# Attention and MLP in one kernel: attention's PSUM in two pools, one copy for eight half transposes, scores in two tasks

## The chip, the cores and the metric

The kernel runs on one core of a Trainium2 chip. The metric is the time of one execution on the device, in microseconds, as the median of three runs. TensorE (PE) multiplies and transposes into PSUM; VectorE (DVE) and ScalarE (ACT) read PSUM; GpSimd (POOL) works in SBUF only; SyncE (SP) issues the DMAs.

## The reference

Causal attention by blocks of 64 over 8 batches, 8 heads, 576 positions and 64 channels, followed by layer norm and a two-layer MLP with ReLU and a residual, all in float32.

```python
scores = scale * np.matmul(q, k.transpose(0, 1, 3, 2))
mask = block_i >= block_j                      # blocks of 64
attn = softmax(np.where(mask, scores, -1e9))   # rows, sum + 1e-9
x = np.matmul(attn, v).transpose(0, 2, 1, 3).reshape(B, S, H * D)
xn = (x - mu) / np.sqrt(var + 1e-06) * g_ln
return x + np.maximum(xn @ w_ch1, 0.0) @ w_ch2
```

## The kernel before

**Tiling.** Attention works on 32 pairs of heads (`pair(k)`). Of a pair's 576 positions the first 64 are done apart, for eight pairs together (`first(m)`, four times). The other 512 make four query blocks of 128, numbered 1 to 4, whose keys reach to 64(2i+1) columns: 192, 320, 448 and 576. Blocks 1 and 2 form the low part, blocks 3 and 4 the high part.

**One pair, step by step** (lines of the profile). `scores1` multiplies the low blocks of both heads into two PSUM tiles `s1` of 512 columns; `scores0` the high blocks into two tiles `s` of 1024 columns, `sab` (L426). `soften` (L444) has VectorE add the mask, scale and take the row minimum out of PSUM into SBUF (`pu` for the low blocks, `pab` for the high ones), and ScalarE the exponential with its sum (L447). `turn` (L457) has TensorE transpose eight cells of 128 x 128 in halves of 64 rows: 16 instructions, the upper halves into one `tr` tile, the lower into another. A pair has three such groups: one from `pu`, two from `pab` (h = 0 and 1). `turned_to` copies each of the two tiles (512 columns) to SBUF as `pt`, by an instruction that the planner gives to VectorE (L237) or ScalarE (L235). `pv` (L469, L473) multiplies with the values into a PSUM tile `o` of 512 columns, in two steps: 4.5 for the low part, 5 for the high one. VectorE transposes `o` out (L536, the output read-out).

**PSUM.** One pool, tag `tr`, has four tiles of one bank that `tr`, `s1`, `o` and later the products `p` share. The other has two tiles `s` of two banks, and gives its place to the second layer's `y` when attention is over.

**Order.** A planner (`Plan`) goes through all tasks in an assumed time, with costs from tables, and gives each free engine the ready task with the lowest priority number; what it emits is the order on the chip, where each engine takes its instructions strictly in that order. For TensorE's part of attention the order is fixed by hand: `pe(at, phase, ...)` files a task under a pair and a phase, and `plan.chain` strings them up by these numbers. Transposes and value steps of pair k stand at k + 1, behind the scores of pair k + 1. `TURN` is the planner's cost of two half transposes.

**The rest of the work.** Beside attention run the decoding of the weights (`decode`, L351 to L379: ScalarE, VectorE, GpSimd and DMAs), layer norm of the first tiles (`norm_tiles`) and the making of the MLP's operands. After attention the MLP follows in 5 rounds of 8 groups: seven products (`products`, L873) and the second layer (`second`, L935) for each.

Of the kernel before, what the change touches and what calls it, by code (L numbers as in the profile page):

```python
# [26 lines left out]
TURN = .112  # L27
# [31 lines left out]
class Plan:  # L59
# [34 lines left out]
    def run(self):  # L94
# [27 lines left out]
        while events:  # L122
# [19 lines left out]
            for eng, heap in ready.items():  # L142
# [3 lines left out]
                while heap:  # L146
# [28 lines left out]
                    k.eng, k.cost, k.done = eng, cost, True  # L175
# [27 lines left out]
def attn_mlp_kernel(ctx: ExitStack, tc: tile.TileContext, qk, qk0, v, v0, w1, w2, g, out):  # L203
# [18 lines left out]
    psum = ctx.enter_context(tc.tile_pool(name="psum", bufs=1, space=PSUM))  # L222
# [802 lines left out]
```

## Time and profile before

| | us |
|---|---|
| three runs | 1059.27, 1056.75, 1055.28 |
| median | 1056.75 |
| profiled execution | 1059.55 |
| its span, first to last instruction | 1057.5 |
| TensorE busy in the span | 1019.6 |
| VectorE, ScalarE, GpSimd busy | 752.7, 515.0, 292.1 |

The profile gives each instruction's start and duration, and for idle time the engine that ended it. A matmul's recorded duration includes its way through the array, so the next one starts before it ends: what a group costs TensorE is the distance from its first start to the next group's first start. The same holds, to a lesser degree, on VectorE and ScalarE.

### The profile page before, as it was taken

Reading aid. Unit: us, or ns where it says so; the run is one execution under the profiler, and the core shown is the slowest. Engines: PE = TensorE matmul, PEld = TensorE weight load, DVE = VectorE, ACT = ScalarE, POOL = GpSimd, SP = SyncE. Lnnn points to the kernel's source line nnn. Section 1 sums busy time; section 2 is a strip of 40 time slices with the busy share of each in tenths; the row PEclk is TensorE's granted clock in tenths of the full one; section 3 lists DMA queues with packets and bytes.
Section 4 is the critical chain, followed back from the end, with each engine's and each line's share of the span. In section 5 each row is a group of like instructions: output and inputs, shape, how many; then the busy total and the mean of one; then the engine's idle time right before and its main releaser. Section 6 shows DMA issues by size and latency. Waiting matters only on the chain.

```text
span 1057.5 us, 19502 instructions
## 1 busy us (share of the span) xinstructions
PE 1019.6 (96%) x7032; PEld 835.2 (79%) x7032; DVE 752.7 (71%) x1636; ACT 515.0 (49%) x1251; POOL 292.1 (28%) x476
## 2 busy tenths in 40 slices
PE   8998998978999999999999999999999999999998
PEld 6776776756677888878888888888888888888997
DVE  6979899988888887894665694665585565465554
ACT  7989898779784643441433251343242422222221
POOL 0323355525245754440222250222231120000000
PEclk9999999989999999999999999999999999999999
DMA  8778798878779999757687657678657767426873
GB/s 273 252 250 261 201 283 260 237 229 300 253 230 311 324 294 270 225 206 255 206 255 219 185 219 256 186 225 263 182 172 260 239 185 237 156 110 233 308 279 125
DMA packets 238688, 248.98 MB, mean 235 GB/s; under 512 B 159488, under 2 KB 189184, under 8 KB 228352
## 3 DMA queue, kind: packets, MB, share of 16 engines
q1 hardware_dynamic: 238592, 247.74, 72.6%
q8 instruction: 55, 0.90, 0.3%
q14 instruction: 41, 0.34, 0.1%
HBM read 182.68 MB, written 65.01 MB: 234 GB/s over the span
## 4 chain that ended last, share of the span: by engine, by line
PE 74%; DVE 12%; ACT 5%; DMA 4%; issue 3%; POOL 2%; SPq 1%; DVEq 0%; POOLq 0%; ACTq 0%
PE y L935 35%; PE p L873 31%; PE o L473 4%; ACT pu L447 2%; DVE pab L444 2%; PE o L469 2%; PE s L426 2%; ACT pt L235 1%; DMA wcs<-wd 1%; DVE pt L237 1%; DVE pu L444 1%; DMA raw<-qk 1%; DVE sgn L360 1%; DVE xm L771 1%; PE tr L457 1%
## 5 line engine op out<-in xcount | busy, mean ns | idle before, releaser
L935 PE MATMUL y<-wc,h 128*128 128x512 f32 (+1 forms) x1740 | 434.5, 388 | 0.9 <-DVE h L893 0.8
L935 PEld LDWEIGHTS y<-wc,h 128*128 128x128 f32 x1740 | 323.0, 188 | 67.3 <-DVE h L893 2.5
L947 DVE TENSOR_TENSOR ya<-y,ya 128x512 f32<-128x512 f32 x290 | 197.9, 684 | 188.9 <-PE y L935 186.7
L873 PE MATMUL p<-xm,wa 128*128 128x512 f32 (+1 forms) x960 | 222.3, 368 | 0.5 <-ACT pt L235 0.5
L873 PEld LDWEIGHTS p<-xm,wa 128*128 128x128 f32 x960 | 169.7, 188 | 32.3 <-ACT pt L235 0.8
L873 PE MATMUL p<-xm,wb 128*128 128x512 f32 (+1 forms) x720 | 166.8, 368 | 0.0
L892 ACT ACTIVATE h<-t 128x512 fp32r<-128x512 f32 (+1 forms) x120 | 62.2, 579 | 175.5 <-DVE t L886 175.4
L881 ACT COPY t<-p 128x512 f32<-128x512 f32 (+1 forms) x120 | 65.3, 544 | 167.0 <-PE p L873 166.8
L873 PEld LDWEIGHTS p<-xm,wb 128*128 128x128 f32 x720 | 127.5, 188 | 23.8 <-issue 0.2
L886 DVE TENSOR_TENSOR t<-p,t 128x512 f32<-128x512 f32 (+1 forms) x120 | 76.3, 636 | 45.9 <-PE p L873 40.9
L426 PE MATMUL s<-raw 64*128 64x224 f32 (+3 forms) x768 | 96.4, 388 | 0.8 <-DVE nm L444 0.5
L447 ACT ACTIVATE pab<-pab,nm 128x576 f32<-128x576 f32 (+1 forms) x128 | 91.5, 723 | 1.1 <-DVE nm L444 0.9
L426 PEld LDWEIGHTS s<-raw 64*128 64x128 f32 x768 | 74.9, 188 | 16.2 <-issue 5.0
L444 DVE CUSTOM_DVE_ANT_0 pab<-s,never 128x576 f32<-128x576 f32 (+1 forms) x128 | 83.4, 682 | 3.0 <-PE s L426 2.3
L473 PE MATMUL o<-pt,v 128*64 128x256 f32 (+1 forms) x768 | 83.2, 352 | 0.0
L473 PEld LDWEIGHTS o<-pt,v 128*64 128x64 f32 x768 | 60.3, 141 | 26.2 <-issue 3.2
L893 DVE SCALAR_TENSOR_TENSOR h<-t,h 128x512 fp32r<-128x512 f32 (+1 forms) x120 | 75.8, 681 | 4.5 <-ACT h L892 4.5
L447 ACT ACTIVATE pu<-pu,nm 128x192 f32<-128x192 f32 (+1 forms) x128 | 63.8, 500 | 30.1 <-DVE nm L444 28.6
L687 POOL TENSOR_SCALAR norm<-norm 128x1 f32<-128x1 f32 x28 | 8.0, 287 | 251.5 <-ACT xn L684 248.9
L457 PE MATMUL tr<-ident,pab 64*128 64x64 f32 x1024 | 53.2, 230 | 24.3 <-ACT pt L235 18.7
L235 ACT COPY pt<-tr 128x512 f32<-128x512 f32 x135 | 71.2, 581 | 2.6 <-PE tr L457 1.2
L354 POOL TENSOR_SCALAR mag<-mag 128x512 f32<-128x512 f32 x32 | 49.9, 1564 | 77.5 <-ACT mag L351 71.7
(95 smaller groups left out, 1027.6 us busy)
## 6 DMA issues: line engine op xcount, KB each, us to landing
wc<-wcs SPq DMA_DIRECT2D x40, 1024.0 KB, 7.0
wa<-was SPq DMA_DIRECT2D x32, 1024.0 KB, 6.6
wb<-wbs SPq DMA_DIRECT2D x32, 768.0 KB, 5.5
raw<-qk SPq DMA_DIRECT2D x31, 576.0 KB, 5.0
wr<-w SPq DMA_DIRECT2D x32, 512.0 KB, 6.2
v<-v SPq DMA_DIRECT2D x32, 320.0 KB, 4.9
x<-xd SPq DMA_DIRECT2D x144, 64.0 KB, 3.8
xrow<-x SPq DMA_DIRECT2D x36, 256.0 KB, 4.0
```

Source lines behind the costliest of these rows:

```text
L235: e.copy(out=out, in_=in_)
L426: nc.tensor.matmul(x, raw.t[HALF[h], 0, col], raw.t[HALF[h], 1, at:at + x.shape[1]], start=True, stop=True)
L444: add("DVE", dve(n) + .01, lambda: nc.vector.tensor_tensor_reduce(out=two(p.t[:, part(i, h)]), in0=mine(), in1=two(hide), scale=-0.125, sc ...
L447: add("ACT", act(n, True) + .14, lambda: nc.scalar.activation(out=p.t[:, part(i, h)], in_=p.t[:, part(i, h)], func=AF.Exp, bias=nm.t[:, at ...
L457: nc.tensor.transpose(to.t[:, 64 * n:64 * n + 64], x[rows], ident[rows, rows])
L473: nc.tensor.matmul(o.t[HALF[h], at + lo:at + 256], v_sb.t[:, ck, HALF[h]], rhs(h), start=False, stop=(n == len(steps) - 1), skip_group_che ...
L873: nc.tensor.matmul(x.t[:, 0:TN], w_(l), xs[m].t[:, 0:half, o, k], start=start and k == e == 0, stop=k == 1 and e == 2, skip_group_check=True)
L881: add("ACT", act(TN), lambda: nc.scalar.copy(out=t.t[:, 0:TN], in_=x.t[:, 0:TN]), r=[r], w=[new], prio=0)
L886: add("DVE", dve(TN), lambda: nc.vector.tensor_add(t.t[:, 0:TN], x.t[:, 0:TN], t.t[:, 0:TN]), r=r, w=[new], prio=0)
L893: add("DVE", dve(TN), lambda: nc.vector.scalar_tensor_tensor(out=x.t[:, 1, 0:TN], in0=src(), scalar=0.0, in1=x.t[:, 0, 0:TN], op0=ALU.max, ...
L935: nc.tensor.matmul(yb.t[:, cut], x.t[:, l, at:at + P], wc.t[:, i, o, cut], start=i == e == 0, stop=i == 1 and e == 2, skip_group_check=end)
L947: add("DVE", dve(cut.stop - cut.start), lambda yb=yb, ya=ya, cut=cut: nc.vector.tensor_add(ya.t[:, cut], yb.t[:, cut], ya.t[:, cut]), r=[p ...
```

## The change

**PSUM.** The pool `tr` becomes `turns`, two tiles of two banks, for `tr`, `s1` and `o`; it lies on the right side of PSUM, the two `s` tiles (`banks`) on the left. `s1` is one tile of 1024 columns with a half for each head. A `tr` tile takes a whole group: the upper halves in its first bank, the lower in its second. `o` uses the first bank of its tile alone. After attention `p` follows on the left and `y` on the right.

**Copies.** `turned_to` empties a group with one instruction of 1024 columns in place of two of 512.

**Scores and order.** `scores0` is split into `scores4` (block 4, 576 columns) and `scores3` (block 3, 448 columns), each of them across both `s` tiles: block 4 takes columns 224 to 800, block 3 those outside. The reductions come in the order 4, 4, 3, 3. The phases are now in `ORDER`: scores of the low blocks, transposes of the former pair's `pu`, block 4, the former pair's two groups of `pab`, block 3; then the value steps as before. `TURN` falls from .112 to .063. `first` takes double tiles likewise, with the same instructions.

```diff
-TURN = .112
+TURN = .063
+ORDER = {"1": 0, "u": 0.1, "4": 0.2, "a": 0.3, "b": 0.4, "3": 0.5}
...
-    psum = ctx.enter_context(tc.tile_pool(name="psum", bufs=1, space=PSUM))
...
-    banks = tc.tile_pool(name="banks", bufs=1, space=PSUM)
-    new_s = kind("s", [P, 1024], F32, 2, banks.__enter__())
+    def region(name, side):
+        return tc.tile_pool(name=name, bufs=1, space=PSUM, side=side)
+    banks = region("banks", "left"), region("turns", "right")
+    new_s = kind("s", [P, 1024], F32, 2, banks[0].__enter__())
 
     class Again:
 
 
-        pool = None
+        def __init__(self, n):
+            self.n, self.pool = n, None
 
         def tile(self, *args, **kw):
             if self.pool is None:
-                banks.__exit__(None, None, None)
-                self.pool = ctx.enter_context(tc.tile_pool(name="banks_y", bufs=1, space=PSUM))
+                banks[self.n].__exit__(None, None, None)
+                self.pool = ctx.enter_context(region(f"again{self.n}", ("left", "right")[self.n]))
             return self.pool.tile(*args, **kw)
-    new_y = kind("y", [P, 512], F32, 4, Again())
+    new_p = kind("p", [P, 512], F32, 4, Again(0))
+    new_y = kind("y", [P, 512], F32, 4, Again(1))
     steps = {}
-    new_tr, new_s1, new_o, new_p = (kind(n, [P, 512], F32, 4, psum, "tr") for n in ("tr", "s1", "o", "p"))
+    turns = banks[1].__enter__()
+    new_tr, new_s1, new_o = (kind(n, [P, 1024], F32, 2, turns, "tr") for n in ("tr", "s1", "o"))
...
-                    for rows, to in zip(HALF, o):
-                        nc.tensor.transpose(to.t[:, 64 * n:64 * n + 64], x[rows], ident[rows, rows])
+                    for z, rows in enumerate(HALF):
+                        nc.tensor.transpose(o.t[:, 512 * z + 64 * n:512 * z + 64 * n + 64], x[rows], ident[rows, rows])
             return go
 
         def turned_to(pt, at, o, x, to):
-            for q, src in enumerate(o):
-                x.append(Buf(parent=pt))
-                evac(lambda q=q: to()[..., 64 * q:64 * q + 64],
-                     lambda src=src: src.t.rearrange("p (c i q) -> p c i q", c=4, q=64), 512, r=[src], w=[x[-1]], prio=at)
+            x.append(Buf(parent=pt))
+            evac(lambda: to().rearrange("p n (z q) -> p z n q", z=2),
+                 lambda: o.t.rearrange("p (z n q) -> p z n q", z=2, q=64), 1024, r=[o], w=[x[-1]], prio=at)
...
-        s1 = [new_s1(), new_s1()]
+        s1 = new_s1()
         nm = new_nm()
         pu = new_pu()
 
         def scores1():
-            a, b = (x.t for x in s1)
+            a, b = s1.t[:, 0:512], s1.t[:, 512:1024]
             mm(2, a[:, 0:320], b[:, 0:320])
             mm(1, a[:, 320:512], b[:, 320:512])
-        pe(k, 0, 512 * 4 / 2400 + .04, scores1, r=[early], w=s1, prio=pr(), mode=64)
+        pe(k, ORDER["1"], 512 * 4 / 2400 + .04, scores1, r=[early], w=[s1], prio=pr(), mode=64)
         low = [[], []]
-        for h, s in enumerate(s1):
-            for n, (i, lo, hi) in enumerate(((2, 0, 320), (1, 320, 512))):
-                low[h].append(soften(pu, s, nm, 4 + 2 * h + n, i, h, lo))
+        for h in range(2):
+            for n, (i, lo) in enumerate(((2, 0), (1, 320))):
+                low[h].append(soften(pu, s1, nm, 4 + 2 * h + n, i, h, 512 * h + lo))
 
         sab = [new_s(), new_s()]
         pab = big_of[k, 0] = new_pab()
 
-        def scores0():
+        def scores4():
             a, b = (x.t for x in sab)
             mm(4, a[:, 224:512], b[:, 224:512])
             mm(4, a[:, 512:800], b[:, 512:800], skip=288)
+
+        def scores3():
+            a, b = (x.t for x in sab)
             mm(3, a[:, 0:224], b[:, 0:224])
             mm(3, a[:, 800:1024], b[:, 800:1024], skip=224)
-        pe(k, 1, 1024 * 4 / 2400 + .06, scores0, r=[early, late], w=[*sab, ends.setdefault(k, Buf())], prio=pr(), mode=64)
+        s4, s3 = [Buf(parent=x) for x in sab], [Buf(parent=x) for x in sab]
+        pe(k, ORDER["4"], 576 * 4 / 2400 + .03, scores4, r=[early, late], w=s4, prio=pr(), mode=64)
+        pe(k, ORDER["3"], 448 * 4 / 2400 + .03, scores3, r=[early, late], w=[*s3, ends.setdefault(k, Buf())], prio=pr(), mode=64)
         done = [[], []]
-        for h, s in enumerate(sab):
-            for n, i in enumerate((4, 3)):
-                done[h].append(soften(pab, s, nm, 2 * h + n, i, h, 224))
+        for n, i, s in (0, 4, s4), (1, 3, s3):
+            for h in range(2):
+                done[h].append(soften(pab, s[h], nm, 2 * h + n, i, h, 224))
         pt0 = big_of[k, 1] = new_pt0()
         final[k] = [*done[0], *done[1]]
         got = []
 
         for h in range(2):
-            o = [new_tr(), new_tr()]
+            o = new_tr()
             cells = [x for c in range(3) for x in ((3, h, c + 1), (4, h, c + 1))] + [(3 + h, h, 0), (4, h, 4)]
             slots = lambda cells=cells: [pab.t[:, cell(*x)] for x in cells]
             need = [*done[h], done[1 - h][1 - h]]
-            pe(k + 1, 3, 8 * TURN, turn(o, slots), r=list(dict.fromkeys(need)), w=o, alloc=[pt0], prio=pr(), mode=64)
-            turned_to(pt0, pr(), o, got, lambda h=h: pt0.t[:, h])
+            pe(k + 1, ORDER["ab"[h]], 8 * TURN, turn(o, slots), r=list(dict.fromkeys(need)), w=[o], alloc=[pt0], prio=pr(), mode=64)
+            turned_to(pt0, pr(), o, got, lambda h=h: pt0.t[:, h].rearrange("p c i n -> p (c i) n"))
...
-        o = [new_tr(), new_tr()]
+        o = new_tr()
         cells = [x for h in range(2) for x in ((1, h, 1), (2, h, 1), (1 + h, h, 0), (2, h, 2))]
         slots = lambda: [pu.t[:, cell(*x)] for x in cells]
-        pe(k + 1, 2, 8 * TURN, turn(o, slots), r=[*low[0], *low[1]], w=o, alloc=[pt1], prio=pr(), mode=64)
-        turned_to(pt1, pr(), o, got, lambda: pt1.t.rearrange("p h c i n -> p (h c) i n"))
+        pe(k + 1, ORDER["u"], 8 * TURN, turn(o, slots), r=[*low[0], *low[1]], w=[o], alloc=[pt1], prio=pr(), mode=64)
+        turned_to(pt1, pr(), o, got, lambda: pt1.t.rearrange("p h c i n -> p (h c i) n"))
...
-        add("DVE", dve(512), lambda: nc.vector.transpose(ot.t, ob.t), r=part_o, w=[ot], prio=pr())
+        add("DVE", dve(512), lambda: nc.vector.transpose(ot.t, ob.t[:, 0:512]), r=part_o, w=[ot], prio=pr())
...
-        s, e, nm = [new_tr(), new_tr()], new_e0(), new_nm()
+        s, e, nm = new_tr(), new_e0(), new_nm()
...
-        o, ot, ots = [new_o(), new_o()], new_ot0(), []
+        o, ot, ots = new_o(), new_ot0(), []
```

Lines of the new kernel stand five to nine below the old ones: L431 is the scores, L462 the transposes, L473 and L477 the value steps, L449 the reductions, L545 the output read-out, L882 the products.

TensorE, pair 7, from its scores to the first value step of pair 6. `s_1019`, `s_1020` and `s_953` are `s1` tiles; `s` are the tiles of the high blocks; `x4` counts equal rows. Before:

```order
L426 MATMUL s_1019<-raw 128x320
L426 MATMUL s_1020<-raw 128x320
L426 MATMUL s_1019<-raw 128x192
L426 MATMUL s_1020<-raw 128x192
L426 MATMUL s<-raw 128x288 x4
L426 MATMUL s<-raw 128x224 x4
L457 MATMUL tr<-ident,pu 128x64 x16
L457 MATMUL tr<-ident,pab 128x64 x32
L469 MATMUL o<-pt_1052,v 64x256 x2
```

and now:

```order
L431 MATMUL s_953<-raw 128x320 x2
L431 MATMUL s_953<-raw 128x192 x2
L462 MATMUL tr<-ident,pu 128x64 x16
L431 MATMUL s<-raw 128x288 x4
L462 MATMUL tr<-ident,pab 128x64 x32
L431 MATMUL s<-raw 128x224 x4
L473 MATMUL o<-pt_967,v 64x256 x2
```

The scores of block 4 and block 3 now stand on the two sides of the former pair's `pab` transposes, and the `pu` transposes ahead of both.

The same place now, with the semaphores that each row waits for (Activation is ScalarE), from block 4 to the first value step:

```order
L431 MATMUL s<-raw 128x288 x4
L462 MATMUL tr<-ident,pab 128x64 [waits DVE_49,Activation_49]
L462 MATMUL tr<-ident,pab 128x64 x11
L462 MATMUL tr<-ident,pab 128x64 [waits Activation_49]
L462 MATMUL tr<-ident,pab 128x64 x3
L462 MATMUL tr<-ident,pab 128x64 [waits Activation_49]
L462 MATMUL tr<-ident,pab 128x64 x15
L431 MATMUL s<-raw 128x224 [waits DVE_49] x2
L431 MATMUL s<-raw 128x224 x2
L473 MATMUL o<-pt_967,v 64x256 [waits DMAHW4_49,Activation_49]
```

The first two rows of block 3 (64 x 224) wait for VectorE, which reads block 4 in the same tiles; the value step waits for a ScalarE copy.

VectorE, from pair 7's high reductions (`pab`) to the output read-out (L536). The `ISA nm` rows read the minimum out. Before:

```order
L444 ISA pab,nm<-s,never 128x576
L444 ISA nm 128x1
L444 ISA pab,nm<-s,never 128x448
L444 ISA nm 128x1
L444 ISA pab,nm<-s,never 128x448
L444 ISA nm 128x1
L237 COPY pt_1079<-tr 128x8x64
L444 ISA pab,nm<-s,never 128x576
L444 ISA nm 128x1
L237 COPY pt_1079<-tr 128x8x64
L536 STREAM_TRANSPOSE ot<-o 128x512
```

and now:

```order
L449 ISA pab,nm<-s,never 128x576
L449 ISA nm 128x1
L449 ISA pab,nm<-s,never 128x576
L449 ISA nm 128x1
L237 COPY pt_1003<-tr 128x2x8x64
L449 ISA pab,nm<-s,never 128x448
L449 ISA nm 128x1
L449 ISA pab,nm<-s,never 128x448
L449 ISA nm 128x1
L365 SCALAR_TENSOR_TENSOR sgn<-wr,sgn 128x512
L368 SCALAR_TENSOR_TENSOR sgn<-mag,sgn 128x512
L545 STREAM_TRANSPOSE ot<-o 128x512
```

Two copies of one bank stood behind three or four of the reductions; one copy of two banks now stands between the two reductions of 576 and the two of 448 columns. The output read-out follows behind them as before, here with two decoding steps (L365, L368) ahead of it.

TensorE at the end of attention, from pair 31's last scores. Before:

```order
L426 MATMUL s<-raw 128x224 x4
L457 MATMUL tr<-ident,pu 128x64 x16
L457 MATMUL tr<-ident,pab 128x64 x16
L873 MATMUL p<-xm_2150,wa 128x512 x6
L457 MATMUL tr<-ident,pab 128x64 x16
L469 MATMUL o<-pt_4731,v 64x256 x2
L473 MATMUL o<-pt_4731,v 64x256 x2
L473 MATMUL o<-pt_4731,v 64x128 x2
```

and now:

```order
L431 MATMUL s<-raw 128x224 x4
L882 MATMUL p<-xm_2069,wa 128x512 x6
L473 MATMUL o<-pt_4440,v 64x256 x2
L477 MATMUL o<-pt_4440,v 64x256 x2
L477 MATMUL o<-pt_4440,v 64x128 x2
L473 MATMUL o<-pt_4477,v 64x256 x2
L477 MATMUL o<-pt_4477,v 64x256 x6
L477 MATMUL o<-pt_4477,v 64x128 x2
L462 MATMUL tr<-ident,pu 128x64 x16
```

The first product `p` stood between two groups of `pab` transposes; it now stands straight behind block 3 of pair 31 and ahead of pair 30's value steps.

## Rows read from the trace of the kernel before

**Rows 1.** The page's busy times: us, share of the span, instructions, by engine.

```profile
PE 1019.6 (96%) x7032; PEld 835.2 (79%) x7032; DVE 752.7 (71%) x1636; ACT 515.0 (49%) x1251; POOL 292.1 (28%) x476
```

**Rows 2.** Busy time by stretch: stretch, length, PE, PEld, DVE, ACT, POOL, clock, DMA, GB/s.

```profile
18.50:299.30 280.80, 250.56 (x3290) 196.14 (x3288) 246.47 (x725) 238.66 (x658) 108.22 (x139) 0.98 0.80 253
299.30:322.30 23.00, 22.50 (x222) 16.17 (x220) 18.79 (x40) 17.61 (x42) 13.60 (x10) 1.00 0.74 235
322.30:1057.50 735.20, 730.83 (x3388) 610.58 (x3384) 477.13 (x836) 246.14 (x519) 169.58 (x322) 1.00 0.70 228
```

**Rows 3.** TensorE's timeline (start, us, instructions): scores of pair 2 and pair 31.

```profile
18.50 2.86 PE L426 MATMUL s<-raw 64*128 64x320 f32 x24
...
299.31 2.86 PE L426 MATMUL s<-raw 64*128 64x320 f32 x24
```

**Rows 4.** TensorE's timeline, one undisturbed pair; idle time before and releaser in brackets.

```profile
101.01 2.86 PE L426 MATMUL s<-raw 64*128 64x320 f32 x24
103.70 0.66 PE L457 MATMUL tr<-ident,pu 64*128 64x64 f32 x16
104.20 0.67 PE L457 MATMUL tr<-ident,pab 64*128 64x64 f32 x16
105.50 0.27 PE L457 MATMUL tr<-ident,pab 64*128 64x64 f32 x1 [0.64 <-ACT pt L235]
105.99 0.70 PE L457 MATMUL tr<-ident,pab 64*128 64x64 f32 x15 [0.21 <-ACT pt L235]
106.62 0.65 PE L469 MATMUL o<-pt,v 128*64 128x256 f32 x4
...
107.78 0.65 PE L469 MATMUL o<-pt,v 128*64 128x256 f32 x4
...
109.87 0.69 PE L574 MATMUL tr<-qk 64*64 64x64 f32 x32
```

**Rows 5.** TensorE's waits, 18.5 to 299.3 us: us in total, times, longest.

```profile
PE tr L457 <- ACT pt L235: 18.1, 37, 3.6
PE o L469 <- ACT pt L235: 4.0, 11, 0.7
PE tr L457 <- DVE nm L444: 2.9, 6, 0.7
```

**Rows 6.** Timeline of all engines, two stretches: VectorE's reductions, decoding, copies.

```profile
28.53 0.49 DVE L444 CUSTOM_DVE_ANT_0 pu<-s,never 128x320 f32<-128x320 f32 x1 [0.34 <-PE s L426]
...
29.91 0.69 DVE L360 SCALAR_TENSOR_TENSOR sgn<-wr,sgn 128x512 int32<-128x512 int32 x1
...
30.51 0.75 DVE L444 CUSTOM_DVE_ANT_0 pab<-s,never 128x576 f32<-128x576 f32 x1
...
115.93 0.75 DVE L444 CUSTOM_DVE_ANT_0 pab<-s,never 128x576 f32<-128x576 f32 x1
...
116.61 0.62 DVE L444 CUSTOM_DVE_ANT_0 pab<-s,never 128x448 f32<-128x448 f32 x1
...
117.70 0.69 DVE L237 COPY pt<-tr 128x512 f32<-128x512 f32 x1
...
118.30 0.75 DVE L444 CUSTOM_DVE_ANT_0 pab<-s,never 128x576 f32<-128x576 f32 x1
```

**Rows 7.** The same timeline: ScalarE's copies and exponentials.

```profile
104.89 1.52 ACT L235 COPY pt<-tr 128x512 f32<-128x512 f32 x3
...
107.08 0.58 ACT L235 COPY pt<-tr 128x512 f32<-128x512 f32 x1
...
108.21 0.77 ACT L447 ACTIVATE pab<-pab,nm 128x576 f32<-128x576 f32 x1
...
108.97 0.67 ACT L447 ACTIVATE pab<-pab,nm 128x448 f32<-128x448 f32 x1
...
109.62 0.68 ACT L351 ACTIVATE mag<-wr 128x512 f32<-128x512 f32 x1
```

**Rows 8.** VectorE's longest wait, 18.5 to 299.3 us: us in total, times, longest.

```profile
DVE ot L536 <- PE o L473: 28.1, 17, 4.1
```

More of the change, by code (lines that the diff above doesn't have):

```diff
@@ L174, in run @@
                         cost, mode = cost + SWITCH[k.mode], k.mode
-                    k.eng, k.cost, k.done = eng, cost, True
+                    k.eng, k.cost, k.done, k.t0 = eng, cost, True, now
                     fn()
@@ L574, in first @@
         pe(8 * m + 4, -1, .6, lambda: by_quarter(lambda a, u, f, t, cols, at: nc.tensor.matmul(
-            s[u].t[t, at], q0.t[f, a, 0], q0.t[f, a, 1], start=True, stop=True, skip_group_check=True)),
-            r=[q0], w=s, alloc=[e], prio=pr(), mode=2)
+            s.t[t, 512 * u + at.start:512 * u + at.stop], q0.t[f, a, 0], q0.t[f, a, 1], start=True, stop=True, skip_group_check=True)),
+            r=[q0], w=[s], alloc=[e], prio=pr(), mode=2)
         load(P * 2048, lambda: nc.sync.dma_start(out=v_0.t.rearrange("p (a n) -> p a n", n=64), in_=v0[m]), w=[v_0], prio=prio)
@@ L582, in first @@
             add("DVE", dve(256), lambda u=u: nc.vector.tensor_reduce(
-                out=nm.t[:, 4 * u:4 * u + 4], in_=ev(s[u].t[:, 0:256]), op=ALU.max, axis=AX.X), r=[s[u]], w=[m1], prio=pr())
-            add("DVE", dve(256), lambda u=u, bc=bc: nc.vector.tensor_sub(side(u), ev(s[u].t[:, 0:256]), bc()),
-                r=[s[u], m1], w=[d1], prio=pr())
+                out=nm.t[:, 4 * u:4 * u + 4], in_=ev(s.t[:, 512 * u:512 * u + 256]), op=ALU.max, axis=AX.X), r=[s], w=[m1], prio=pr())
+            add("DVE", dve(256), lambda u=u, bc=bc: nc.vector.tensor_sub(side(u), ev(s.t[:, 512 * u:512 * u + 256]), bc()),
+                r=[s, m1], w=[d1], prio=pr())
             d.append(d1)
@@ L604, in first @@
         pe(8 * m + 5, 2.5, 4 * .112, across, r=[pn], w=[tr], alloc=[pt], prio=pr())
-        evac(lambda: pt.t, lambda: tr.t, 512, r=[tr], w=[turned_], prio=pr())
-        o, ot, ots = [new_o(), new_o()], new_ot0(), []
+        evac(lambda: pt.t, lambda: tr.t[:, 0:512], 512, r=[tr], w=[turned_], prio=pr())
+        o, ot, ots = new_o(), new_ot0(), []
         def values():
@@ L614, in values @@
                         nc.tensor.matmul(
-                            o[u].t[HALF[h], 0:256].rearrange("p (t c q) -> p t c q", t=2, q=32)[:, :, c],
+                            o.t[HALF[h], 512 * u:512 * u + 256].rearrange("p (t c q) -> p t c q", t=2, q=32)[:, :, c],
                             v_0.t[HALF[u], at], pt.t[HALF[u], at].rearrange("p (t q) -> p t q", q=32), start=True, stop=True,
                             skip_group_check=True)
-        pe(8 * m + 5, 5.5, .6, values, r=[turned_, v_0], w=o, alloc=[ot], prio=pr(), mode=2)
+        pe(8 * m + 5, 5.5, .6, values, r=[turned_, v_0], w=[o], alloc=[ot], prio=pr(), mode=2)
         for u in range(2):
             ots.append(Buf(parent=ot))
-            add("DVE", dve(256), lambda u=u: nc.vector.transpose(half(ot, u), o[u].t[:, 0:256]), r=[o[u]], w=[ots[u]], prio=pr())
+            add("DVE", dve(256), lambda u=u: nc.vector.transpose(half(ot, u), o.t[:, 512 * u:512 * u + 256]), r=[o], w=[ots[u]], prio=pr())
         x0parts[m] = []
```

## The prediction

> **What bounds the kernel now.** I read the page's busy table first (TensorE 96%, the others far less [rows 1]), then the busy time by stretch, then TensorE's rows of one undisturbed pair, its waits, and last the rows of VectorE and ScalarE that release it. The run has two stages. From 322 us on TensorE is busy for 730.8 of 735.2 us [rows 2] with the products and second-layer sums, which the edit leaves as they are; nothing is to be won there. The attention stage is where TensorE is held up. Scores of pair 2 start at 18.50 us and of pair 31 at 299.31 us; 30 such rows, so 29 periods of 280.8 / 29 = 9.68 us on average [rows 3]. Of these 29 distances 11 are up to 9.0 us, 8 more up to 9.6, and 10 longer.
>
> In an undisturbed pair [rows 4] the scores take 103.70 - 101.01 = 2.69 us of issue, 16 transposes 0.50 us (103.70 to 104.20), the two value steps 1.16 us (106.62 to 107.78) and 2.09 us (107.78 to 109.87). With three groups of transposes that is 2.69 + 1.50 + 1.16 + 2.09 = 7.44 us of work in a period of 8.86: 1.42 us are lost, all of them between 104.70 and 106.62, where the second `pab` group waits for copies out of PSUM. The waits say the same of the whole stage: 18.1 us of transposes waiting for ScalarE's copies, 4.0 us of value steps waiting for them, 2.9 us for VectorE's reductions [rows 5].
>
> But TensorE is not alone. In the same 280.8 us it is busy 250.6 us, VectorE 246.5 and ScalarE 238.7 [rows 2]: 8.64, 8.50 and 8.23 us a period. So three engines at 85 to 89% hold each other up, and a TensorE stall that goes is worth only what the other two can follow.
>
> **The change, part by part.** I call the groups of transposes u (from `pu`), a and b (from `pab`), and the scores s1, s4 (576 columns) and s3 (448).
>
> *One copy in place of two.* Three ScalarE copies of 512 take 1.52 us together, one alone 0.58 [rows 7], so they follow each other every (1.52 - 0.58) / 2 = 0.47 us; an exponential of 576 columns is followed after 0.76 us (108.21 to 108.97) and one of 448 after 0.65 (to 109.62) [rows 7], 0.11 us for 128 columns. A copy of 1024 is then an estimated 0.47 + 4 x 0.11 = 0.91 us, against 0.94 for two. VectorE: a 512 copy takes 0.60 us from its start to the next, the 576 reduction 0.68 and each 448 one 0.545 [rows 6]; at about 1.05 ns a column, 1024 is about 1.13 us against 1.20. The program's lists hold 131 ScalarE and 61 VectorE copies before, 71 and 25 after. ScalarE: 131 x 0.47 = 61.6 to 71 x 0.91 = 64.6 us, no gain. VectorE: 61 x 0.60 = 36.6 to 25 x 1.13 = 28.3 us, a gain of 8.3 us, 0.26 us a pair. The 1024 source spans two banks; the 576 reduction does so already (columns 224 to 800 of its tile), at the rate of the 448 one, so I add nothing for that. The copy starts later, after all 16 transposes, and lasts 0.91 to 1.13 us where two copies ran side by side in about 0.6; that costs about 0.4 us at each place where TensorE is next in line.
>
> *The new order hides that.* Per column the scores take 2.69 / 1536 = 1.75 ns, so s1 is 0.90, s4 1.01 and s3 0.78 us. Put a pair together by hand, t = 0 when s1(k) starts. s1 to 0.90, u to 1.40, s4 to 2.41. VectorE reads out the former pair's output from 0.1 to 0.8 (512 columns, counted as a 512 copy with its hand-over; it stands ahead of the reductions in the order), starts the four `pu` reductions at 1.10 when s1 has ended, is through at 2.48 (four take 29.91 - 28.53 = 1.38 us [rows 6]) and releases s1's banks at 2.6. a then runs 2.6 to 3.1: 0.2 us lost. ScalarE copies u from 1.6 to 2.5, so b has its banks at 3.1 and runs to 3.6. s3 writes the outer columns of the two banks whose inner columns the two 576 reductions read; the order shows it waiting for VectorE there. These run from 2.6 to 4.0, so s3 is held from 3.6 to 4.05: 0.45 us lost, and ends at 4.83. ScalarE's copy of a (3.5 to 4.4) and VectorE's of b (4.05 to 5.2) are both done when the value steps want them (4.83 and 5.99), which end at 8.08. So 1.42 us of loss becomes 0.64, and 8.86 becomes 8.08.
>
> *What keeps that from coming through whole.* ScalarE needs 8.23 us a period and loses no work, so an undisturbed pair cannot run below about 8.25: the 11 short periods gain 0.6 us each, 6.6 us. The 8 middle ones, with VectorE or ScalarE late by less than an operation, I give 0.5 us: 4.0. The 10 long ones are filled by other work on VectorE (layer norm, weight decoding, the first-block task) and gain what VectorE itself sheds, 0.26 us: 2.6. Together 13.2 us.
>
> *The two pools.* s1, the transposes and the output share two double banks instead of four single ones, so the output tile, which needs one bank, now holds two, and u waits for the former pair's output to be read out. In the hand schedule that is done at 0.8, before u is due at 0.90, so it costs nothing; if VectorE is one operation late (0.60 us for a decoding step, from 29.91 to 30.51 [rows 6]) it costs 0.5 us in that pair. The middle periods' 0.5 us, in place of 0.78, already allow for such a delay in every second one.
>
> *The end of attention.* Products now live where the scores were, so the first product must wait until pair 31's last 448 reductions are read, and the order puts it straight behind s3(31), ahead of the value steps that could run: two reductions of 0.545 us and about 0.3 us of hand-over, 1.4 us lost. Before, that stretch lost 0.5 us in all (22.50 busy of 23.00 [rows 2]). I take 1.4 lost; the bounds are 0.5 (later gaps shrink by as much) and 3 (a copy ahead of the reductions).
>
> *Nothing else.* The first-block task gets a double tile for each pair of single ones: same instructions, four times in all. Changes of tile shape on TensorE stay at two a pair, since s1 to s3 and all transposes use 64 rows. TensorE's granted clock was 0.98 in the stage [rows 2]; fewer stalls might win back the 2%, at most some 2.5 us of its 250 us of work if half of it lies beside other waits; I take nothing.
>
> **The sum** is made against the profiled execution, 1059.55 us (its span 1057.5 and about 2 us around it): 1059.55 - 13.2 + 1.4 = 1047.7. The median of the three runs, 1056.75, lies 2.8 us below that execution, so 1047.7 - 2.8 = 1045 us, a gain of 1.1%.
>
> **Rivals.**
> 1. *The rest follows too, 1033 us.* If the removed stalls also shorten the middle and long periods by 0.78, the gain is 29 x 0.78 = 22.6 us, plus 2 us of clock, less 1.4: 1056.75 - 23.2 = 1033.5. For it: VectorE stood still for 28.1 us of the stage with the output read-out waiting for value steps [rows 8], which is slack. Against it: ScalarE's 8.23 us a period.
> 2. *ScalarE is the bound, 1054 us.* Its work does not shrink, and at 85% busy with waits on both sides it may already set the mean. Then only a part of the 8.3 us that VectorE sheds shows, say a third: 1056.75 - 2.8 = 1054. Against it: in the undisturbed pair TensorE waits for ScalarE in one burst, not all along.
> 3. *VectorE's queue drives TensorE, 1070 us.* The place is the loop output read-out, four reductions, two 576 reductions, copy of b, value step: by the schedule 5.2 + 2.09 = 7.3 us if nothing else sits in it, since s3 can no longer be written while its banks are read. VectorE's other work averages 8.50 - 0.26 - 4.5 (0.60 + 1.38 + 1.36 + 1.13) = 3.7 us a pair, of which 1.1 is the 448 reductions. Whatever of it is queued inside that loop is paid by TensorE. It decides from 9.68 - 7.3 = 2.4 us a pair; at 2.85 us it costs 0.45 x 29 = 13 us: 1070. Against it: the order mostly puts decoding after the 448 reductions, where TensorE is in the value steps. No row here shows TensorE writing to a bank that another engine reads. The Trainium skill, "PSUM — Partial Sum Buffer", section "PSUM bank collisions raise a hardware error", says to guard PSUM by bank, not by address: two engines in one bank at once is an error, whatever the columns. By that rule splitting the scores over the same two banks gives no early write, and the time is this rival's 1070; if s3 could run beside the reductions, this rival would lose its loop and half its chance.
>
> **How the numbers follow.** Forecast 50% (1037 to 1051), rival 1 15% (1027 to 1037), rival 2 15% (1051 to 1058), rival 3 20% (1061 to 1080). A measurement of this kernel tells about 0.5% from no change, 5.3 us, so faster means below 1051.5: 50 + 15 and a fifth of rival 2, 68%. Within 0.5% is the rest of rival 2, 12%; slower 20%. The range leaves out 5% below and 15% above: 1029 to 1064. Its lower end is rival 1 with more clock regained, its upper end the start of rival 3.
>
> **What would show it.** In the profile of the changed kernel: 30 rows of s1 at a mean distance of 9.2 us; in an undisturbed pair a short wait (0.2 us) of a, one of s3 for VectorE's reductions (0.45 us), and none of the value steps; transposes waiting for ScalarE's copies down from 18 us to under 6; copies of 1024 at about 1.0 us (ScalarE) and 1.2 us (VectorE) recorded; VectorE's copies 8 us less in all; a wait of 1 to 2 us ahead of the first product. I am wrong if the waits of u, a and s3 for VectorE add up to more than the 25 us they replace (rival 3), if ScalarE shows no idle time in the stage (rival 2), or if the products' stage, 735 us, does not simply move forward because its weights or rows come late.

## The result: 1.0% faster, and the profile after

The changed kernel takes 1046.23 us (median of four runs, 1045.03 to 1046.90) against 1056.37 us for the kernel before on the same chip: ratio 0.9899, 95% interval 0.9877 to 0.9921. Its profiled execution has a span of 1044.7 us, 12.8 us shorter than before. TensorE's work is the same, VectorE is busy 8.0 us less [rows 1]:

```profile
PE 1018.1 (97%) x7032; PEld 819.9 (78%) x7032; DVE 744.7 (71%) x1607; ACT 515.9 (49%) x1188; POOL 288.2 (28%) x472
```

The same three stretches as in [rows 2], cut at the scores of pair 2 and of pair 31 (stretch, length, PE, PEld, DVE, ACT, POOL, clock, DMA, GB/s), and the two rows of TensorE's timeline that answer to [rows 3]:

```profile
17.42:280.40 262.98, 247.82 (x3290) 179.66 (x3288) 234.76 (x687) 235.60 (x599) 96.49 (x128) 0.99 0.82 260
280.40:304.20 23.80, 22.45 (x224) 16.54 (x222) 18.11 (x38) 16.56 (x35) 11.61 (x11) 1.00 0.65 235
304.20:1044.70 740.50, 733.21 (x3384) 612.11 (x3382) 481.69 (x848) 251.53 (x525) 179.44 (x329) 1.00 0.71 230
```

```profile
17.42 1.14 PE L431 MATMUL s<-raw 64*128 64x320 f32 x8
...
280.40 1.13 PE L431 MATMUL s<-raw 64*128 64x320 f32 x8
```

Pair 2 starts 1.1 us earlier, the 29 periods last 263.0 us where they lasted 280.8, and from the scores of pair 31 to the end it is 764.3 us where it was 758.2: 1.1 + 17.8 - 6.1 = 12.8 us. Attention gained more than the whole kernel, and a third of that was lost behind it.

TensorE's timeline of an undisturbed pair (its period is 70.27 - 61.96 = 8.31 us), as [rows 4]:

```profile
61.96 1.13 PE L431 MATMUL s<-raw 64*128 64x320 f32 x8
62.93 0.66 PE L462 MATMUL tr<-ident,pu 64*128 64x64 f32 x16
63.42 1.19 PE L431 MATMUL s<-raw 64*128 64x288 f32 x8
64.76 1.22 PE L462 MATMUL tr<-ident,pab 64*128 64x64 f32 x32
65.78 1.38 PE L431 MATMUL s<-raw 64*128 64x224 f32 x8
67.09 0.65 PE L473 MATMUL o<-pt,v 128*64 128x256 f32 x4
...
70.27 1.13 PE L431 MATMUL s<-raw 64*128 64x320 f32 x8
...
74.08 1.02 PE L431 MATMUL s<-raw 64*128 64x224 f32 x8
75.03 0.65 PE L473 MATMUL o<-pt,v 128*64 128x256 f32 x4
```

No row has an idle time in brackets, yet two groups were held. Block 3's scores take 67.09 - 65.78 = 1.31 us here and 75.03 - 74.08 = 0.95 in the next pair: the wait for the second 576 reduction lies between the matmuls of the group, and only the distance to the next group shows it. TensorE's waits from 18 to 290 us (in total, times, longest), as [rows 5]:

```profile
PE tr L462 <- DVE nm L449: 5.8, 8, 1.8
PE tr L462 <- DVE e L593: 2.1, 4, 0.7
PE s L431 <- DVE ot L545: 1.9, 6, 0.7
PE p L882 <- DVE nm L449: 1.2, 1, 1.2
...
PE tr L462 <- ACT pt L235: 0.9, 4, 0.4
```

The 18.1 us of transposes waiting for ScalarE's copies are 0.9 us. Of the 6.1 us lost later 0.8 lie in the second stretch (23.80 us in place of 23.00), in which the first product waits 1.2 us. The other 5.3 us have one place, the end of the MLP's first round. The timeline of all engines there:

```profile
447.17 1.29 DVE L780 TENSOR_TENSOR xm<-xt,xm 128x256 fp32r<-128x256 f32 x2
...
448.38 0.95 DVE L769 TENSOR_TENSOR tt<-xt,tt 128x256 f32<-128x256 f32 x1
...
449.25 1.55 DVE L237 CAST xm<-tt 128x256 fp32r<-128x256 f32 x2
...
450.73 3.47 DVE L902 SCALAR_TENSOR_TENSOR h<-t,h 128x512 fp32r<-128x512 f32 x3
...
453.12 4.63 PE L944 MATMUL y<-wc,h 128*128 128x512 f32 x10 [3.55 <-DVE h L902]
```

The second layer waits 3.55 us for `h`, which stands on VectorE behind steps that make the second round's operands. The stretches of the wait and of the ten matmuls behind it:

```profile
450.50:453.10 2.60, 0.00 (x0) 0.00 (x0) 2.60 (x4) 0.19 (x1) 2.60 (x4) 0.85 0.93 394
453.10:457.55 4.45, 4.43 (x10) 3.44 (x11) 4.45 (x8) 1.41 (x4) 4.05 (x5) 0.50 0.50 212
```

The ten run at a granted clock of 0.50, 443 ns each where six took 1.36 us, 227 ns each, before the wait: 2.2 us more. The clock stays at 0.50 up to 459.1 us, and four products behind them start 427 ns apart as well, some 0.8 us more.

### The profile page after: what moved, and what is told of

The parts are those of the page before. It is cut to its first block, busy times and chain, and to the rows that moved or that the text cites. A ratio compares the mean times of both kernels' runs of the same rounds, so it can differ in the third digit from the quotient of the medians.

```text
span 1044.7 us, 19419 instructions
## 1 busy us (share of the span) xinstructions
PE 1018.1 (97%) x7032; PEld 819.9 (78%) x7032; DVE 744.7 (71%) x1607; ACT 515.9 (49%) x1188; POOL 288.2 (28%) x472
## 4 chain that ended last, share of the span: by engine, by line
PE 82%; DVE 8%; ACT 3%; SPq 2%; DMA 2%; issue 2%; POOL 1%; DVEq 0%; POOLq 0%; ACTq 0%
PE y L944 37%; PE p L882 32%; PE o L477 4%; PE s L431 4%; PE tr L462 3%; ACT pt L235 2%; PE o L473 2%; DVE pab L449 2%; SPq L675 1%; DVE pu L449 1%; DMA v<-v 1%; DVE ot L545 1%; DMA wcs<-wd 1%; DMA x<-xd 0%; ACT pab L452 0%
## 5 line engine op out<-in xcount | busy, mean ns | idle before, releaser
L882 PE MATMUL p<-xm,wa 128*128 128x512 f32 (+1 forms) x960 | 222.1, 369 | 1.2 <-DVE nm L449 1.2
L882 PEld LDWEIGHTS p<-xm,wa 128*128 128x128 f32 x960 | 170.5, 189 | 33.3 <-DVE nm L449 1.6
L882 PE MATMUL p<-xm,wb 128*128 128x512 f32 (+1 forms) x720 | 166.3, 368 | 0.0
L882 PEld LDWEIGHTS p<-xm,wb 128*128 128x128 f32 x720 | 127.5, 188 | 23.9 <-DVE t L895 0.2
L431 PE MATMUL s<-raw 64*128 64x288 f32 (+3 forms) x768 | 115.4, 401 | 3.4 <-DVE ot L545 1.9
L452 ACT ACTIVATE pab<-pab,nm 128x448 f32<-128x448 f32 (+1 forms) x128 | 90.7, 712 | 2.3 <-DVE nm L449 2.2
L431 PEld LDWEIGHTS s<-raw 64*128 64x128 f32 x768 | 73.6, 190 | 20.3 <-issue 4.1
L449 DVE CUSTOM_DVE_ANT_0 pab<-s,never 128x448 f32<-128x448 f32 (+1 forms) x128 | 82.9, 685 | 7.1 <-PE s L431 6.4
L235 ACT COPY pt<-tr 128x1024 f32<-128x1024 f32 (+1 forms) x75 | 73.7, 985 | 22.3 <-PE tr L462 20.8
L477 PE MATMUL o<-pt,v 128*64 128x256 f32 (+1 forms) x768 | 80.3, 344 | 0.0
L477 PEld LDWEIGHTS o<-pt,v 128*64 128x64 f32 x768 | 55.4, 137 | 28.0 <-issue 0.4
L902 DVE SCALAR_TENSOR_TENSOR h<-t,h 128x512 fp32r<-128x512 f32 (+1 forms) x120 | 73.4, 662 | 4.1 <-ACT h L901 4.1
L452 ACT ACTIVATE pu<-pu,nm 128x320 f32<-128x320 f32 (+1 forms) x128 | 64.2, 505 | 4.5 <-DVE nm L449 4.4
L462 PEld LDWEIGHTS tr<-ident,pab 64*128 64x128 f32 x1024 | 36.2, 140 | 24.3 <-ACT pt L235 15.6
```

The costliest lines, as they stand in the source:

```text
L235: e.copy(out=out, in_=in_)
L431: nc.tensor.matmul(x, raw.t[HALF[h], 0, col], raw.t[HALF[h], 1, at:at + x.shape[1]], start=True, stop=True)
L449: add("DVE", dve(n) + .01, lambda: nc.vector.tensor_tensor_reduce(out=two(p.t[:, part(i, h)]), in0=mine(), in1=two(hide), scale=-0.125, sc ...
L452: add("ACT", act(n, True) + .14, lambda: nc.scalar.activation(out=p.t[:, part(i, h)], in_=p.t[:, part(i, h)], func=AF.Exp, bias=nm.t[:, at ...
L462: nc.tensor.transpose(o.t[:, 512 * z + 64 * n:512 * z + 64 * n + 64], x[rows], ident[rows, rows])
L477: nc.tensor.matmul(o.t[HALF[h], at + lo:at + 256], v_sb.t[:, ck, HALF[h]], rhs(h), start=False, stop=(n == len(steps) - 1), skip_group_che ...
```

## The experiments

My theory at first was the prediction's: the new order brings the gain. Rival A was the merged copy, rival B the planner's cost `TURN`, which the prediction had not costed. All ratios are to the kernel before on the same chip; the last two columns, in us, are from the profiled executions. Each is one execution; those of before, e1, e3 and e12 took 2.1 to 4.7 us more than the median of their kernel.

| kernel | ratio, 95% interval | scores of pair 2 to 31 | from there to the end |
|---|---|---|---|
| before | 1 | 280.8 | 758.2 |
| changed | 0.9899, 0.9877 to 0.9921 | 263.0 | 764.3 |
| e1 two copies | 1.0148, 1.0119 to 1.0177 | 292.3 | 766.6 |
| e2 scores together | 1.0006, 0.9993 to 1.0020 | 274.9 | 764.6 |
| e3 cost .112 | 0.9995, 0.9963 to 1.0028 | 283.0 | 757.9 |
| e4 before, cost .063 | 0.9924, 0.9898 to 0.9950 | 270.6 | 761.6 |
| e5 single banks | 1.0003, 0.9988 to 1.0018 | 270.3 | 768.1 |
| e6 cost .085 | 0.9917, 0.9888 to 0.9946 | 263.8 | 767.8 |
| e7 block 3 first | 0.9931, 0.9908 to 0.9953 | 270.4 | 760.1 |
| e8 operands dear | 0.9892, 0.9863 to 0.9922 | 263.5 | 763.5 |
| e9 h first | 0.9856, 0.9834 to 0.9877 | 263.2 | 761.2 |
| e10 before, cost .07 | 1.0007, 0.9993 to 1.0022 | 277.8 | 762.8 |
| e11 before, cost .10 | 0.9994, 0.9977 to 1.0011 | 277.4 | 760.1 |
| e12 cost .07 | 0.9919, 0.9895 to 0.9943 | 268.6 | 765.1 |

### One part undone: copies, order, cost

**e1**, the merge undone:

```diff
-            evac(lambda: to().rearrange("p n (z q) -> p z n q", z=2),
-                 lambda: o.t.rearrange("p (z n q) -> p z n q", z=2, q=64), 1024, r=[o], w=[x[-1]], prio=at)
+            for z in range(2):
+                x.append(Buf(parent=pt))
+                evac(lambda z=z: to()[..., 64 * z:64 * z + 64],
+                     lambda z=z: o.t[:, 512 * z:512 * z + 512].rearrange("p (n q) -> p n q", q=64), 512, ...)
```

> The changed kernel with the merge alone undone: each group of transposes is emptied by two copies of 512 columns, one for each bank of its double tile; order and pools stay. My theory (the order brings the gain): 1046 to 1050 us, since ScalarE's step was 0.94 us for two copies against an estimated 0.91 for one and only VectorE gets its 8 us back on its list; transposes waiting for ScalarE stay under 6 us. Rival A (the merged copy brings the gain): 1054 to 1058 us, the time of the kernel before.

1073.48 us, 1.5% slower than before: worse than either theory. VectorE's waits and TensorE's (total, times, longest) say why:

```profile
DVE pt L237 <- ACT pt L235: 22.1, 39, 1.0
...
PE tr L462 <- DVE pt L237: 22.6, 28, 1.6
```

Where the two copies of a group go to different engines, the second waits for the first: both read one tile, though another bank of it. With two tiles of one bank, as before, VectorE's copies show no such wait. The granted clock of the stage was 0.96, where the changed kernel has 0.99. So the run undoes more than the merge; it shows that a double tile wants one copy, not what one copy is worth.

**e2**, the order undone:

```diff
-ORDER = {"1": 0, "u": 0.1, "4": 0.2, "a": 0.3, "b": 0.4, "3": 0.5}
+ORDER = {"1": 0, "4": 0.1, "3": 0.2, "u": 0.3, "a": 0.4, "b": 0.5}
```

> The changed kernel with the order alone undone: the two score tasks of the high blocks follow the low scores directly, then the three groups of transposes, then the value steps; merged copies and both pools stay. My theory: the three groups need three double tiles and there are two, so the loss of 1.42 us a pair stays and the longer copy adds up to 0.4: 1056 to 1066 us, transposes waiting for ScalarE 18 us or more. Rival A (the merged copy brings the gain): 1045 to 1050 us.

1059.23 us, no gain, and transposes waited 14.6 us for ScalarE (total, times, longest):

```profile
PE tr L462 <- ACT pt L235: 14.6, 21, 1.2
```

That is near what my theory had (18 us or more), and rival A falls in the form that I gave it. But attention was 274.9 us, shorter than before, so something else in the change does help.

**e3** and **e4**, the cost alone, in the changed kernel and in the one before:

```diff
-TURN = .063
+TURN = .112
```

> The changed kernel with the planner's cost of the transposes alone put back to .112; the order of TensorE is the same, what VectorE and ScalarE take when may differ. My theory: 1045 to 1049 us. Rival B (the gain comes from the planner's new cost, which deals out VectorE's and ScalarE's work otherwise): 1054 to 1058 us.

```diff
-TURN = .112
+TURN = .063
```

> The kernel before with the planner's cost of the transposes alone set to .063. My theory: 1054 to 1060 us, no change, since the place where TensorE waits for copies stays. Rival B: 1045 to 1050 us.

Both went against my theory: 1059.33 us without the cost, 1051.17 us with the cost alone. The eight executions of e3 scatter widely, from 1053.01 us at a mean granted clock of 1.000 to 1065.26 us at 0.990, so its 283.0 us of attention is one of several values that the same program can take. A group of 16 transposes is 8 x .112 = 0.90 us in the planner's time by the old cost and 0.50 by the new one, and 0.50 on the chip [rows 4]. What follows is seen in an undisturbed pair of e4 (TensorE's, VectorE's and ScalarE's timeline):

```profile
71.00 2.86 PE L426 MATMUL s<-raw 64*128 64x320 f32 x24
...
74.19 0.67 PE L457 MATMUL tr<-ident,pab 64*128 64x64 f32 x16
75.08 0.94 PE L457 MATMUL tr<-ident,pab 64*128 64x64 f32 x16 [0.22 <-ACT pt L235]
...
79.25 2.86 PE L426 MATMUL s<-raw 64*128 64x320 f32 x24
...
73.89 0.76 DVE L444 CUSTOM_DVE_ANT_0 pab<-s,never 128x576 f32<-128x576 f32 x1
74.58 1.28 DVE L237 COPY pt<-tr 128x512 f32<-128x512 f32 x2
...
74.46 1.04 ACT L235 COPY pt<-tr 128x512 f32<-128x512 f32 x2
```

The planner's time for a group is now the chip's. It puts two copies on VectorE behind the first 576 reduction; in the kernel before, the two 448 reductions stood ahead of VectorE's copy, and three copies were queued on ScalarE [rows 7]. The second `pab` group starts 75.08 - 71.00 = 4.08 us into the pair, against 105.50 - 101.01 = 4.49 [rows 4], and the period is 79.25 - 71.00 = 8.25 us against 8.86: in the old order 0.61 of the 1.42 us are gone that I had the new order remove. In the whole stage transposes wait 12.6 us for ScalarE's copies, where it was 18.1.

In e3 the planner's slow transposes do the reverse. VectorE's and TensorE's timeline of an undisturbed pair (period 91.45 - 82.66 = 8.79 us):

```profile
82.66 1.13 PE L431 MATMUL s<-raw 64*128 64x320 f32 x8
...
85.22 0.69 DVE L365 SCALAR_TENSOR_TENSOR sgn<-wr,sgn 128x512 int32<-128x512 int32 x1
85.83 0.75 DVE L449 CUSTOM_DVE_ANT_0 pab<-s,never 128x576 f32<-128x576 f32 x1
...
86.50 0.75 DVE L449 CUSTOM_DVE_ANT_0 pab<-s,never 128x576 f32<-128x576 f32 x1
...
86.64 1.70 PE L431 MATMUL s<-raw 64*128 64x224 f32 x8
88.27 0.65 PE L473 MATMUL o<-pt,v 128*64 128x256 f32 x4
...
91.45 1.14 PE L431 MATMUL s<-raw 64*128 64x320 f32 x8
```

A decoding step of 0.61 us stands ahead of the 576 reductions. That the planner, with its slower transposes, saw a gap there is my reading of its cost; the trace shows only the step. Block 3's scores, held by the second reduction, take 88.27 - 86.64 = 1.63 us: 0.32 more than in the changed kernel and 0.68 more than unheld. The program has 16 decoding steps in this place with .112, 2 with .063. This accounts for the short pairs alone: by length, e3's 11 shortest take 4.3 us more than the changed kernel's, its 10 longest 13.7 of the 20.0 us.

### Is it the cost, or any new plan?

Each cost gives another order of VectorE's and ScalarE's work in all of attention, so a gain could be a lucky draw. **e6**, **e10**, **e11** and **e12** change the same number, `TURN`, to .085 and .07 in the changed kernel, to .07 and .10 in the one before.

> The changed kernel with the planner's cost of the transposes at .085, between .063 and .112. In its program only 2 decoding steps stand between the low reductions and the second 576 reduction, as with .063; with .112 there are 16. If the cost acts through what it queues in that loop: 1044 to 1050 us, as with .063. If it acts in proportion to the error of the planned time: about 1052 us, half of the way to 1059.

> The kernel before with the planner's cost of the transposes at .07. If the gain of .063 on this structure (ratio 0.992) comes from planned times that are near the chip's: 0.990 to 0.995. If each plan is a draw whose time scatters by some 10 us whatever the cost: anything from 0.985 to 1.005.

> The kernel before with the planner's cost of the transposes at .10, near the .112 it had. By the planned times: 0.997 to 1.002. By scatter: anything from 0.985 to 1.005.

> The changed kernel with the planner's cost at .07. By the planned times: 0.988 to 0.992, as with .063 and .085. By scatter: anything from 0.985 to 1.003.

The changed kernel gives 0.990 to 0.992 with three costs from .063 to .085 and 0.9995 with .112: a gain at each of the three, and not in proportion to the error of the planned time, as the loop theory of e6 had it. On the kernel before, e11 gave what planned times let expect, and e10 did not: .07 gave 1.0007 where .063 gave 0.9924. Its undisturbed pairs are as short as e4's (8.24 us). What differs are a few long ones. Three of them, of the kernel before, of e10 and of the changed kernel (columns as above):

```profile
206.84:221.57 14.73, 11.12 (x110) 8.29 (x105) 10.19 (x29) 9.03 (x24) 8.66 (x18) 0.77 0.91 330
```

```profile
140.86:155.81 14.95, 11.36 (x106) 8.10 (x105) 9.76 (x31) 8.97 (x26) 9.62 (x22) 0.77 0.99 331
```

```profile
176.47:188.63 12.16, 9.82 (x105) 6.79 (x105) 10.14 (x31) 9.90 (x24) 8.87 (x12) 0.86 0.59 187
```

Each holds one long wait of TensorE (3.6, 2.7 and 1.8 us) and a granted clock of 0.77 to 0.86 in the mean; it is 1.00 in the undisturbed pairs. e10 has two pairs of 15 and 16 us, the changed kernel none over 12.2. Which single step makes such a stall in one plan and not in the next was not isolated.

So the two structures have to be compared at the same cost. Scores of pair 2 to pair 31, us:

| `TURN` | before's banks, copies, order | changed |
|---|---|---|
| .112 | 280.8 | 283.0 (e3) |
| .07 | 277.8 (e10) | 268.6 (e12) |
| .063 | 270.6 (e4) | 263.0 |

With a cost near the chip's the structure takes 7.6 and 9.2 us off attention, with the old cost nothing. In whole times the step is clear at .07 (1.0007 to 0.9919); at .063 it is 0.9924 to 0.9899, with intervals that overlap, since a part is lost behind attention. Each figure is also one execution with its own clock. The stage of e4 (columns as above):

```profile
17.82:288.40 270.58, 250.25 (x3290) 196.54 (x3288) 244.82 (x723) 232.49 (x644) 102.00 (x134) 0.97 0.81 254
```

Its clock record has 13.6 us at 0.50, the changed kernel's stage 3.4 us. Taking half of such time as lost, some 5 of the 7.6 us are clock by this estimate; at .07, with 13.6 us in e10 and 10.2 in e12, some 1.7 of the 9.2.

### Does the order need the double banks?

**e5** puts the two score tasks, the new order and the cost .063 on the four single banks with two copies a group:

```diff
-        pe(k, 1, 1024 * 4 / 2400 + .06, scores0, r=[early, late], w=[*sab, ends.setdefault(k, Buf())], ...)
+        pe(k, ORDER["4"], 576 * 4 / 2400 + .03, scores4, r=[early, late], w=s4, ...)
+        pe(k, ORDER["3"], 448 * 4 / 2400 + .03, scores3, r=[early, late], w=[*s3, ends.setdefault(k, Buf())], ...)
```

> The kernel before with the planner's cost .063, the scores in two tasks and the new order, but with its four single banks, two copies a group and products in the same pool. If the order brings its gain by itself: 1044 to 1049 us, below the 1051 of the cost alone. If it needs the merged copy (rival A in its new form: a group's one tile is free after one instruction): 1051 us or more, with transposes or scores waiting for copies.

1058.61 us, as the second expectation had it: attention 270.3, as e4 without the order (270.6), and 6.5 us more behind it, where the second layer waits for `h` again (7.7 us in e5, 2.6 in e4). e2, double banks without the order, had 274.9. Only both together gave 263.0, one plan each.

### Two smaller questions

**e7** exchanges blocks 3 and 4 in `ORDER` and in the reductions' order:

```diff
-ORDER = {"1": 0, "u": 0.1, "4": 0.2, "a": 0.3, "b": 0.4, "3": 0.5}
+ORDER = {"1": 0, "u": 0.1, "3": 0.2, "a": 0.3, "b": 0.4, "4": 0.5}
```

> The changed kernel with the two score tasks exchanged: block 3 (448 columns) early, block 4 (576) behind the transposes, the reductions in the order 3, 3, 4, 4. Two 448 reductions end some 0.27 us before two 576 ones, so the second task should not be held. If the hold of the second score task sets the undisturbed pair: 8.31 becomes about 8.0 us, and the time 1041 to 1045 us. If ScalarE or VectorE's queue sets it: 1045 to 1048 us; worse than that if the planner queues other work in the loop (the program shows 8 decoding and weight steps there, not 2).

1050.19 us. The undisturbed pair does become shorter, 8.15 us, but transposes wait for ScalarE's copies again (11.9 us in 29 waits): the exchange took 0.16 us off such a pair (0.3 expected), and what this plan lost elsewhere was more.

**e8** and **e9** go for the 6 us lost behind attention. e8 makes VectorE's subtractions dearer to the planner for the second round (`DVE=dve(256) + .5 * (n == 1)`); e9 lets that round's later operands wait for `h`:

```diff
-    def operands(n, prio):
+    def operands(n, prio, late=()):
...
-            pr = prio + .1 * step + .01 * q
+            pr, r = prio + .1 * step + .01 * q, [*r, *(late if step > 1 else ())]
...
+                 [x for h in before[2][0].values() for x in h[1]] if n == 1 else ())
```

> The changed kernel with the planner's cost of the subtractions that make the second round's operands raised by 0.5 us on VectorE, so that GpSimd gets more of them; four of VectorE's steps ahead of the h of the first round's last group are gone. If the 3.55 us of waiting at 453 us and the half clock behind it are what the products' stage lost: 1040 to 1043 us. If the work comes late from GpSimd instead: 1045 us or more, with products waiting for operands.

> The changed kernel, in which the second round's operands from the third group on wait for the h of the first round's last group, so that VectorE has nothing of them queued ahead of that h. If the 3.55 us of waiting at 453 us and the ten matmuls at half clock behind it (2.2 us) were the loss of the products' stage: about 5 us less, a ratio near 0.985, no wait of y for h over 0.7 us, and no second wait behind it. If the operands then come late: a wait of the second round's products for xm, and a ratio of 0.989 or more.

e8 is inconclusive: the wait shrank to 2.8 us, and the ratio of 0.9892 can't be told from the changed kernel's. e9 measured 1043.81 us, ratio 0.9856, the fastest of all (its interval and the changed kernel's touch at 0.9877). All engines' timeline and TensorE's waits of e9 at that place:

```profile
447.29 3.32 PE L944 MATMUL y<-wc,h 128*128 128x512 f32 x12
447.52 2.44 DVE L902 SCALAR_TENSOR_TENSOR h<-t,h 128x512 fp32r<-128x512 f32 x3 [0.70 <-ACT h L901]
```

```profile
PE p L882 <- DVE xm L780: 1.7, 2, 1.1
PE p L882 <- POOL xm L780: 0.3, 1, 0.3
```

`h` comes before the second layer runs out of work, the clock stays at 1.00, and 2.0 us of waiting for operands take the place of 3.55 + 2.2 + 0.8. From the scores of pair 31 to the end it is 761.2 us in place of 764.3; by the ratios the gain is 0.43% (4.5 us), by the two profiled spans 2.8 us. Both expectations of e9 hold in part: the loss was there, and some of it turned into the wait for operands.

## Why the prediction was right in its number and not in its reasons

1045 us was forecast and 1046.2 measured. Step by step:

- **The cost `TURN` was not priced.** This is the step that failed. The prediction goes through copies, order, pools and tail and ends the list with "nothing else"; the planner's cost stands in the diff and in no term. e3 and e4 show that without it nothing is gained, and that alone it brings most of it in this one plan (0.9924 of 0.9899), though nothing at .07 (e10, 1.0007). The cost came in unseen all the same: VectorE's order, from which the pair was put together, had been made with it.
- **The cause of the stall.** "The new order hides that" named the undisturbed pair's 1.42 us. e4 removes 0.61 of it (8.86 to 8.25) in the old order; the changed kernel ends at 8.31, no better. In the undisturbed pair the structure brings nothing once the cost is right; 6.5 of its 7.6 us and 6.2 of its 9.2 lie in the 18 longer pairs.
- **The pair put together by hand** held: 8.08 us, raised to 8.25 for ScalarE's limit, and 8.31 measured. The limit itself did not show: e7's undisturbed pair takes 8.15 us, and in the pair above ScalarE stands idle for 0.43 us until the transposes come. `a` was held for VectorE by some 0.33 us (64.76 - 63.42 = 1.34 for 1.01 us of block 4), forecast 0.2; block 3 by 0.36, forecast 0.45; value steps waited 0.2 us in the whole stage. The Trainium skill, "PSUM — Partial Sum Buffer", section "PSUM bank collisions raise a hardware error", has PSUM guarded by bank and not by address. The hold agrees with it, since VectorE read other columns of the same banks; the wait is the program's own, and no run takes it away.
- **The terms of the periods**, the 29 distances between starts, ranked by length on both sides: the 11 short ones gained 6.4 us (forecast 6.6), the 8 middle ones 4.2 (4.0), the 10 long ones 7.2 (2.6). The last was mis-sized, in part by the clock, for which I had taken nothing, against "some 2.5 us" as the most. Two long pairs of before (14.73 and 11.69 us, mean clock 0.77 and 0.85) ran partly at half clock, 10.2 us in all; the changed kernel's stage has 3.4 us of it, by the same estimate 3.4 us less lost.
- **Copies**: 1008 ns on ScalarE in the mean and 1221 on VectorE recorded (1.0 and 1.2 forecast), VectorE's busy time down 8.0 us (8.3). **First product**: 1.21 us of waiting for pair 31's reductions (1.4).
- **The products' stage does not simply move forward**, which stood among the signs that the prediction is wrong: 6.1 us were lost. e9, without the stall and the half clock at 453 us, gets 3.1 of them back and pays 2.0 for new waits for operands. The loss hides the 4.6 us by which the long pairs were better than forecast. That the total came out right is luck: two errors cancel.
- **Rivals.** Rival 1's 22.6 us in attention was not far (17.8); the rest ate it. Rival 2 fell: ScalarE's work hardly shrank (235.6 us against 238.7 [rows 2]), and the mean period went from 9.68 to 9.07 us all the same. Rival 3's place was right, and its condition was set by the cost: e3 has the decoding inside the loop, at 1059 us rather than 1070.

## What to carry to other kernels

Where a planner sets the order, a cost table is part of the kernel: compare each cost in it with the measured distance between groups, and price a changed number like a changed instruction. Judge a change of structure at two or three neighbouring costs, since one plan can be off by 7 us and executions of one program (e3) by 12, and a part of a change alone may do nothing. When a stage becomes shorter, look at the next one's first hand-overs: here a third of the gain was lost there.

## What the hardware showed unexpectedly

- **A stall can be paid twice.** After TensorE stood still for 3.55 us, the granted clock was 0.50 for the next 4.45 us (1.2 GHz of 2.4) and ten matmuls took 443 ns each in place of 227. It is not so with each stall: transposes wait equally long for the same reductions in the changed kernel and in e8, and the mean clock of the 6.2 us behind it is 0.72 in the one and 1.00 in the other (TensorE's timeline, then that stretch):

```profile
182.40 0.94 PE L462 MATMUL tr<-ident,pab 64*128 64x64 f32 x16 [1.80 <-DVE nm L449]
...
182.40:188.60 6.20, 6.20 (x56) 4.25 (x56) 4.34 (x11) 4.66 (x14) 3.19 (x4) 0.72 0.41 70
```

```profile
182.74 0.71 PE L462 MATMUL tr<-ident,pab 64*128 64x64 f32 x16 [1.81 <-DVE nm L449]
...
182.71:188.91 6.20, 5.96 (x70) 4.20 (x72) 5.33 (x13) 5.55 (x16) 3.23 (x4) 1.00 0.39 71
```

And in the pair of 11.69 us of the kernel before the clock fell with no wait over 0.65 us:

```profile
258.97:270.66 11.69, 10.33 (x139) 7.65 (x137) 9.96 (x27) 8.99 (x24) 7.63 (x8) 0.85 0.75 268
```

- **VectorE beside GpSimd.** The three `h` steps took 3.47 us while GpSimd was busy all the time, and 2.44 in e9, where it was busy for 1.63 us; their mean over the kernel is 0.72 us. The two stretches:

```profile
450.73:454.20 3.47, 1.08 (x3) 0.83 (x3) 3.47 (x5) 0.52 (x2) 3.47 (x4) 0.73 1.01 427
```

```profile
447.52:449.96 2.44, 2.30 (x10) 1.61 (x9) 2.44 (x4) 2.44 (x7) 1.63 (x2) 1.00 0.24 44
```

Two casts took 1.55 us where such a cast takes 0.29 to 0.37 in the mean. The planner's costs know nothing of that, and the queue ahead of `h` was late by it. The Trainium skill, "SBUF — State Buffer", section "SBUF: two separate sides", says that VectorE, in a step with two SBUF inputs, and GpSimd lock a common pair of ports against each other for a whole instruction; the `h` steps are of that kind, and their 3.47 against 2.44 us agree. The stretches also differ in the DMAs' share (1.01 against 0.24), and no run separates the two.
